# Attention, conv gate and routed attention in one kernel: P V products of both head halves as one operation in the score banks

## The chip, the cores and the metric

The kernel runs on one core of a Trainium2 chip. The metric is the device time in microseconds (us) of one execution. Three runs of the kernel before took 679.58, 679.75 and 681.16 us, so the median is 679.75.

## What is computed

Three stages follow each other, for 8 batches of 576 positions and 512 channels (cut to what matters):

```python
# 1: windowed attention, 8 heads of 64
scores = scale * q @ k.T;  mask = (rel >= 0) & (rel < 64)
attn = exp(scores - max); attn = attn / (attn.sum(-1) + 1e-9);  x = attn @ v
# 2: causal conv of 5 taps as a gate
gate = 1 / (1 + exp(-conv(x, conv_w)));  x = (gate * (x @ w_val)) @ w_out
# 3: four experts of causal attention (64 wide), the two with the largest logits kept
logits = x @ w_gate;  sel = the 2 largest of 4;  w = softmax(sel)
for e in experts:
    a = softmax(causal(scale * (x @ wq[e]) @ (x @ wk[e]).T))
    out += chosen[e] * w[e] * (a @ (x @ wv[e]) @ wo[e])
```

The kernel multiplies `w_out` into `wq`, `wk`, `wv` and `w_gate` beforehand, so stage 3 starts from the gated values.

## The kernel before

A batch is cut into five row tiles, four of 128 positions and a last one of 64. That makes forty tiles, n = 0 to 39, with j = n % 5. Each passes through the same chain of operations, which the code names by short stages:

- `qt`, `qe`: q and k are transposed on TensorE (line 669) and copied out of PSUM.
- `sp`, `mx`, `ex`, `ph`, `pl`: the scores of stage 1 (lines 728, 730), their maximum (737), the exponential (744), and probabilities as a float16 value plus a float16 remainder (`Phl`, lines 275 and 282). `PT` transposes them by DMA.
- `pv`, `xn`: the product with the values (line 794) for four heads at a time, so two halves for each tile of 128 positions and one for a last tile. `rcs` (799) and `rci` (802) make the reciprocals of the sums from column 64, and `xn` (809) multiplies by them.
- `xt`, `xT`, `xh`, `xl`: x is transposed on TensorE (829, 826) and written three ways (275, 842). GpSimd then computes the conv (861 to 872).
- `val`, `gv`, `gh`, `gl`: the product with `w_val` (890 to 892), the gate and the split. `qk` (923 to 925) and `v3` (941 to 943, 954) are the products with the folded weights, `rt` (992 to 1030) the routing.
- `s3`, `m3`, `x3`, `f3`, `ph3`, `pl3`, `P3T`: the scores of stage 3 (1073) in one or two groups, softmax, `P3hl`, DMA transpose (1118). `y` (1153) and `o` (1174, 1178 to 1180) are the two last products, `ot` and `st` the copy and the store.

Every float32 product is made of three float16 ones (high times high, high times low, low times high).

PSUM has eight banks. `sc` has two buffers of two banks for the scores of both stages, `pj` two of one bank for `val`, `qk`, `v3` and `o`, `tr` one bank for the transposes, and `o` one bank that `pv` and `y` share. A buffer is taken at an operation's first matmul and is free again when the last reader is done. For `sc` that is the `pl` or `pl3` residual on VectorE.

The order of instructions on each engine is not that of the code. A planner, the class `Plan`, runs once while the kernel is built: it holds each operation's cost, its readers and the buffers that it takes, and places operations by a due time, which is the tile's start plus the stage's entry in the table `OFF` (with `BOOST`, `EARLY` and others). What results is a fixed order on each engine, with a fixed buffer for each tile; an engine waits at an instruction whose operands are not there. `SP` issues all DMAs, loads, stores and transposes alike. At the start TensorE also gets 36 groups of filler matmuls (line 1201) while the weights load and are converted. The folded weights are scaled and split on VectorE (`sps` at 540 to 542, then the residuals `wproj<-wp,sp,wproj` at 282); `qk` of tile 0 waits for them.

Of the kernel before, what the change touches and what calls it, by code (L numbers as in the profile page):

```python
# [34 lines left out]
OFF = dict(yh=61969.4, x3=76298.1, vl=20442.0, vs=13922.2, qk=54953.8, val=50000.0, ot=20813.6, yn=88307.5, gv=18491.1,  # L35
           qt=454.3, qe=-25419.0, gl=26778.7, rt=99733.5, yl=94279.8, s3=67381.4, ex=47180.1, vh=31559.9, st=81376.7,
           xT=10029.4, dq=13818.2, xl=67807.4, am=-5435.3, ph3=58596.7, xn=-25423.0, v3h=38686.3,
           pl=23451.7, o=98000.0, ph=101124.6, pl3=67418.4, h3=52915.4, yt=64737.1, th=53943.5,
           v3l=14936.7, xt=4442.6, l3=40133.4, m3=74450.1, P3T=76142.0, sp=15925.6, ld=59750.6, pv=28118.3,
           vb=7408.6, cv=66570.7)  # L40
# [8 lines left out]
WATV = 23439.39  # L49
WATP = 61184.73  # L50
# [4 lines left out]
BOOST = {0: 49596.2, 3: 463.2, 4: -4467.5, 5: 1761.0, 7: -1392.4, 8: 4527.3}  # L55
LD0 = -175524.04
LD1 = 1628.22
ORDER = "raw0 wv0 wv3 wv2 v2 v1 v3 v0 v4 wv1 cw wo2 raw1 wo wo1 raw2 wo0 raw3 wcat raw4 wo3".split()
# [11 lines left out]
EARLY = 2.85  # L70
# [147 lines left out]
def attention_conv_moe(ctx: ExitStack, tc: tile.TileContext, q, k, v, w_val, conv_w, w_out,  # L218
# [439 lines left out]
    def attn1(n):  # L658
# [142 lines left out]
        def rci(half):  # L801
            ve.reciprocal(T_["rc", n, half], T_["rc", n, half])

        def xn(half):
            o, rc = T_["o1", n, half], T_["rc", n, half]
# [3 lines left out]
            ve.tensor_mul(dst, o[:, :, 0:64], rc[:, :, None].to_broadcast([128, 4, 64]))  # L809

        vr = [("VA", n, 0), ("VA", n, 1)] + ([("VB", n)] if j else [])
        for h in range(NB):
            op("pv", n, (("PE", (18 if j else 13) * mm(65)),), lambda h=h: pv(h), r=[("PT", n)] + vr, w=[("o1", n, h)])
            chain("xn", n, ("rc", n, h), [("DVE", lambda h=h: rcs(h)), ("DVE", lambda h=h: rci(h))], [("o1", n, h)], [])
            op("xn", n, (("DVE", dv(256)),), lambda h=h: xn(h),
               r=[("o1", n, h), ("rc", n, h, 1)] + ([("xn", n, 0)] if h else []), w=[("xn", n, h)])
# [93 lines left out]
    def proj(n):  # L910
# [73 lines left out]
        op("v3l", n, both(4, False), lg, r=[("pw", n)], w=[("w4", n, 0)])  # L984

        def rtA():
# [44 lines left out]
        op("rt", n, (("DVE", 450.0),), rtA, r=[("pw", n), ("w4", n, 0), ("scs", b, 3)], w=[("pw", n, "c"), ("w4", n, 1)])  # L1031
# [8 lines left out]
    def attn2(n):  # L1040
# [197 lines left out]
```

## Time and profile before

| what | value |
|---|---|
| median of three runs | 679.75 us |
| profiled execution, its own time | 679.55 us |
| span of its trace, first to last instruction | 677.7 us |
| PE (TensorE matmul) busy | 628.5 us, 93% |
| DVE (VectorE) busy | 557.4 us, 82% |
| ACT (ScalarE) busy | 515.6 us, 76% |
| POOL (GpSimd) busy | 483.1 us, 71% |
| DMA queue q1, share of 16 engines | 74.1% |

The ends of matmuls are modelled in the trace, so PE's busy time is an upper figure. PEld is TensorE's loading of weights, which runs beside PE. A wait is put down to the instruction that came last. Idle time of an engine that is not the bound costs nothing.

### The profile page before, as it was taken

To read this page: it belongs to the slowest core of one execution; us is meant where nothing else is said; L and a number is where in the kernel's file an instruction comes from. 1 tells how busy PE (TensorE), PEld (TensorE's weight loads), DVE (VectorE), ACT (ScalarE), POOL (GpSimd) and SP (SyncE) were. 2 spreads that over 40 slices of the span, in tenths; PEclk is the share of its full clock that TensorE was granted. 3 is DMA by queue.
4 is the path that set the end of the run, shared out by engine and by line. 5 is a ranking of instruction groups with operands and counts; after the bars stand their busy time and mean duration, and the time that the engine had idled before them with its cause. 6 is when DMAs were issued, how large, how long until landed. Compare 5 with 4: busy or idle time off the path is not lost. (4 is left out here: it accounts for less than half of the span.)

```text
span 677.7 us, 25338 instructions
## 1 busy us (share of the span) xinstructions
PE 628.5 (93%) x10225; PEld 489.9 (72%) x10237; DVE 557.4 (82%) x1695; ACT 515.6 (76%) x1340; POOL 483.1 (71%) x546
## 2 busy tenths in 40 slices
PE   8979979889999999999989999999999999999985
PEld 4436768677787778777877778777887688767753
DVE  7695697788979988998888886989789898887782
ACT  2656557877897888888797869787897888777773
POOL 4674967997596688786985879497977777973500
PEclk9989989999999999999999999999999999999998
DMA  8769952795995988967996977797686664556257
GB/s 224 188 164 194 235 114 46 163 168 107 157 223 120 173 153 139 196 129 143 162 184 142 180 134 154 156 177 150 114 172 129 96 127 111 98 114 118 43 123 145
DMA packets 306531, 99.45 MB, mean 147 GB/s; under 512 B 294362, under 2 KB 296942, under 8 KB 306414
## 3 DMA queue, kind: packets, MB, share of 16 engines
q1 hardware_dynamic: 306414, 97.84, 74.1%
q8 instruction: 80, 1.31, 0.8%
q14 instruction: 37, 0.30, 0.1%
HBM read 34.63 MB, written 9.44 MB: 65 GB/s over the span
## 5 line engine op out<-in xcount | busy, mean ns | idle before, releaser
L872 POOL TENSOR_TENSOR acc<-acc,ctmp 128x512 f32<-128x512 f32 (+1 forms) x160 | 185.9, 1162 | 6.3
L870 POOL TENSOR_TENSOR ctmp<-xT,cw 128x512 f32<-128x512 f32 (+1 forms) x160 | 151.5, 968 | 0.0
L744 ACT ACTIVATE sc<-sc,mx 128x128 f32<-128x128 f32 x288 | 99.0, 344 | 33.0 <-DVE mx L737 25.0
L890 PE MATMUL pj<-xs,wval 128*128 128x128 f16 (+1 forms) x640 | 101.1, 216 | 1.0 <-ACT k L275 1.0
L923 PE MATMUL pj<-gs,wproj 128*128 128x128 f16 (+1 forms) x640 | 101.6, 216 | 0.1
L924 PE MATMUL pj<-gs,wproj 128*128 128x128 f16 (+1 forms) x640 | 101.4, 216 | 0.0
L925 PE MATMUL pj<-gs,wproj 128*128 128x128 f16 (+1 forms) x640 | 101.4, 216 | 0.0
L891 PE MATMUL pj<-xs,wval 128*128 128x128 f16 (+1 forms) x640 | 101.0, 215 | 0.0
L892 PE MATMUL pj<-xs,wval 128*128 128x128 f16 (+1 forms) x640 | 100.9, 215 | 0.0
L1087 ACT ACTIVATE sc<-sc,mx 128x128 f32<-128x128 f32 (+3 forms) x144 | 75.9, 527 | 30.2 <-DVE mx L1082 27.3
L861 POOL TENSOR_TENSOR acc<-xT,cw 128x512 f32<-128x512 f32 (+1 forms) x31 | 31.7, 1023 | 81.9 <-issue 40.7
L282 DVE SCALAR_TENSOR_TENSOR P3hl<-sc,mx,P3hl 128x128 f16<-128x128 f32 (+3 forms) x144 | 75.8, 573 | 11.6 <-ACT P3hl L275 10.3
L275 ACT ACTIVATE P3hl<-sc,mx 128x256 f16<-128x256 f32 (+4 forms) x134 | 66.4, 564 | 8.9 <-DVE mx L1100 4.9
L1073 PE MATMUL sc<-k,q 64*128 64x128 f32 (+5 forms) x384 | 66.5, 451 | 4.9 <-DVE P3hl L282 3.5
L1082 DVE TENSOR_REDUCE mx<-sc 128x4 f32<-128x512 f32 (+3 forms) x64 | 61.5, 965 | 3.4 <-PE sc L1073 2.6
L923 PEld LDWEIGHTS <-wproj 128*128 128x128 f16 x640 | 62.1, 99 | 2.3 <-issue 0.5
L890 PEld LDWEIGHTS <-wval 128*128 128x128 f16 x640 | 61.9, 99 | 1.7 <-issue 0.9
L891 PEld LDWEIGHTS <-wval 128*128 128x128 f16 x640 | 61.9, 99 | 1.6 <-issue 1.1
L924 PEld LDWEIGHTS <-wproj 128*128 128x128 f16 x640 | 62.1, 99 | 0.5 <-issue 0.3
L925 PEld LDWEIGHTS <-wproj 128*128 128x128 f16 x640 | 62.1, 99 | 0.0
L892 PEld LDWEIGHTS <-wval 128*128 128x128 f16 x640 | 61.9, 99 | 0.0
L691 POOL TENSOR_TENSOR VA<-rv,VA 128x512 f16<-128x512 f32 (+1 forms) x40 | 45.9, 1156 | 19.5 <-ACT VA L275 11.4
(200 smaller groups left out, 1763.4 us busy)
## 6 DMA issues: line engine op xcount, KB each, us to landing
VB<-VA SPq DMA_DIRECT2D x64, 132.0 KB, 2.9
raw<-in_q SPq DMA_DIRECT2D x32, 256.0 KB, 3.9
raw<-in_k SPq DMA_DIRECT2D x32, 256.0 KB, 3.8
rv<-in_v SPq DMA_DIRECT2D x32, 256.0 KB, 3.9
out<-ot SPq DMA_DIRECT2D x32, 256.0 KB, 2.7
w<-in_moe_w_val SPq DMA_DIRECT2D x4, 512.0 KB, 5.2
w<-in_moe_w_out SPq DMA_DIRECT2D x4, 512.0 KB, 3.7
rv<-in_v SPq DMA_DIRECT2D x8, 128.0 KB, 3.5
```

Source lines behind the costliest of these rows:

```text
L282: ve.scalar_tensor_tensor(o, i, scale, hi, op0=OP.mult, op1=OP.subtract)
L744: ac.activation(ps[:, i, :], ps[:, i, :], AF.Exp, bias=t[:, hh:hh + 1])
L870: po.tensor_mul(y, x[:, :, t + i:t + i + T], W["cw"][:, :, t + i:t + i + 1].to_broadcast([128, 4, T]))
L872: po.tensor_add(acc[:, :, :T], acc[:, :, :T], y)
L890: pe.matmul(p[:, m, :T], lhsT=w0, rhs=xs[:, 0, c, :T], start=c == 0, stop=False)
L891: pe.matmul(p[:, m, :T], lhsT=w0, rhs=xs[:, 1, c, :T], start=False, stop=False)
L892: pe.matmul(p[:, m, :T], lhsT=w1, rhs=xs[:, 0, c, :T], start=False, stop=c == 3)
L923: pe.matmul(p[:, m, :T], lhsT=w0, rhs=gs[:, 0, c, :T], start=c == 0, stop=False)
L924: pe.matmul(p[:, m, :T], lhsT=w0, rhs=gs[:, 1, c, :T], start=False, stop=False)
L925: pe.matmul(p[:, m, :T], lhsT=w1, rhs=gs[:, 0, c, :T], start=False, stop=c == 3)
L1073: pe.matmul(ps[ot, c0:c0 + r.shape[-1]], lhsT=l, rhs=r, start=bk not in seen, stop=i == final[bk])
L1087: ac.activation(ps[:, x], ps[:, x], AF.Exp, bias=mx[:, x:x + 1], accum_out=mx[:, 4 + x:5 + x])
```

## The change

`pv` becomes one operation for a tile. It takes an `sc` buffer (two banks, 264 columns of one for each half) and issues the matmuls of both halves one after the other. One `rcs` and one `rci` then work on 128x8 sums, and two `xn` multiplications follow. The `o` bank is gone; its bank goes to `tr`, which now has two buffers, and `y` takes one of these. In the routing, `lg` now writes the logits already scaled, two comparisons multiply the raw ones by the same scale, and the `tensor_scalar` that scaled the maximum is gone (40 instructions). With this, most numbers of the planner's tables are new, so almost every engine's order differs.

```diff
-           P3hl=2, P3T=3, V3=7, q3=3, k3=2, ys=2, ot=1, am=2, scs=3, w4=3, sc=2, o=1, tr=1, pj=2,
+           P3hl=2, P3T=3, V3=7, q3=3, k3=2, ys=2, ot=1, am=2, scs=3, w4=3, sc=2, tr=2, pj=2,
-KIND = dict(wf=("pj", 1), kT=("kT", 1), k3=("k3", 1), qp=("tr", 2), s1p=("sc", 1), s3p=("sc", 2), o1=("o", 2), xp=("tr", 1), yp=("o", 1),
+KIND = dict(wf=("pj", 1), kT=("kT", 1), k3=("k3", 1), qp=("tr", 2), s1p=("sc", 1), s3p=("sc", 2), o1=("sc", 1), xp=("tr", 1), yp=("tr", 1),
-ORDER = "raw0 wv0 wv3 wv2 v2 v1 v3 v0 v4 wv1 cw wo2 raw1 wo wo1 raw2 wo0 raw3 wcat raw4 wo3".split()
+ORDER = "wv2 v4 wv3 raw0 v3 wv0 v1 v2 v0 wv1 cw wo2 wo raw1 raw2 wo3 wo1 wo0 raw3 wcat raw4".split()
-EARLY = 2.85
+EARLY = 3.83
...
-            o = bank(("o1", n, half), [128, 4, 66])
+            o = o1(half)
...
-        def rcs(half):
-            o = T_["o1", n, half]
-            T_["rc", n, half] = rc = pool.tile([128, 4], F32, name="rc", bufs=6)
-            ve.tensor_scalar(rc, o[:, :, 64], 1e-9 * PS, 256.0, op0=OP.add, op1=OP.mult)
+        def o1(half):
+            return T_["o1", n][:, 512 * half:512 * half + 264].rearrange("p (i d) -> p i d", d=66)
...
+        def pvs():
+            bank(("o1", n), [128, 1024])
+            for h in range(NB):
+                pv(h)
...
+        def rcs():
+            T_["rc", n] = rc = pool.tile([128, 8], F32, name="rc", bufs=4)
+            ve.tensor_scalar(rc[:, :4 * NB].rearrange("p (h i) -> p h i", h=NB)[:, :, :, None], both_halves(64, 65), 1e-9 * PS, 256.0, op0=OP.add, op1=OP.mult)
...
+        op("pv", n, (("PE", (18 if j else 13) * mm(65) * NB),), pvs, r=[("PT", n)] + vr, w=[("o1", n)])
+        chain("xn", n, ("rc", n), [("DVE", rcs), ("DVE", rci)], [("o1", n)], [])
...
-            copy(e, w4[:, 0], T_["pw", n][:, 128:132])
+            copy(e, w4[:, 0], T_["pw", n][:, 128:132], col(b, 3))
...
-            ve.tensor_tensor(r[:, :, 1], other, own, op=OP.is_equal)
-            ve.tensor_tensor(r[:, :, 0], other, own, op=OP.is_gt)
-            t = w4[:, 3]
-            ve.tensor_reduce(t[:, 0:1], w4[:, 0], axis=AX.X, op=OP.max, negate=True)
-            ve.tensor_scalar(t[:, 0:1], t[:, 0:1], col(b, 3), None, op0=OP.mult)
+            ve.scalar_tensor_tensor(r[:, :, 1], own, col(b, 3), other, op0=OP.mult, op1=OP.is_equal)
+            ve.scalar_tensor_tensor(r[:, :, 0], own, col(b, 3), other, op0=OP.mult, op1=OP.is_lt)
+            ve.tensor_reduce(w4[:, 3, 0:1], w4[:, 0], axis=AX.X, op=OP.max, negate=True)
...
-            o = bank(("yp", n), [128, 2, 128])
+            o = bank(("yp", n), [128, 4, 128])
```

Three places of the order. The first is VectorE around the `xn` of tile 18 (j = 3), before: the two halves stand five rows apart, and each has its own reciprocals.

```order
L799 TENSOR_SCALAR rc<-o 128x4
L802 RECIPROCAL rc<-rc 128x4
L809 TENSOR_TENSOR xn<-o,rc 128x4x64
L282 SCALAR_TENSOR_TENSOR P3hl<-sc,mx_6420,P3hl 128x512 x2
L907 TENSOR_TENSOR gs<-pj,gs 128x512
L799 TENSOR_SCALAR rc<-o 128x4
L282 SCALAR_TENSOR_TENSOR Phl<-sc,Phl 128x512
L802 RECIPROCAL rc<-rc 128x4
L809 TENSOR_TENSOR xn<-o,rc 128x4x64
```

The same tile in the changed kernel reads from an `sc` buffer:

```order
L809 TENSOR_SCALAR rc<-sc 128x8
L277 COPY kT<-tr 128x4x64
L812 RECIPROCAL rc<-rc 128x8
L907 SCALAR_TENSOR_TENSOR pj<-acc,pj 128x512
L818 TENSOR_TENSOR xn<-sc,rc 128x4x64
L282 SCALAR_TENSOR_TENSOR P3hl<-sc,mx_6375,P3hl 128x512 x2
L818 TENSOR_TENSOR xn<-sc,rc 128x4x64
```

One chain of reciprocals serves both halves, and four other VectorE instructions stand between its first step and its last.

The second place is TensorE just before the first `qk` (tile 0). Before, the second half of tile 3's `pv` stands directly ahead of it:

```order
L794 MATMUL o<-VB,PT 64x65
L794 LDWEIGHTS PT
L794 MATMUL o<-VA_105,PT 64x65
L923 LDWEIGHTS wproj
L923 MATMUL pj<-gs,wproj 128x128
```

In the changed kernel the `pv` of tile 5 and transposes for tiles 8 and 9 stand there:

```order
L797 MATMUL sc<-VA_103,PT 128x65
L669 MATMUL tr<-ident,raw 128x128 x4
L669 MATMUL tr<-ident,raw 128x64 x4
L932 LDWEIGHTS wproj
L932 MATMUL pj<-gs,wproj 128x128
```

Ahead of the first `qk` TensorE now has two more `val`, two more `xt`, one more `sp`, five more `qt` and three more halves of `pv`; the filler groups and the weight products ahead of it are the same in number.

The third place is VectorE where the scale of the folded weights is made (540 to 542, `sps`). Before, it follows the `xn` of tile 2's first half:

```order
L593 TENSOR_REDUCE am<-rv 64x1
L809 TENSOR_TENSOR xn<-o,rc 128x4x64
L540 TENSOR_REDUCE cm<-sc 128x2
L541 TENSOR_REDUCE cm<-sc 128x1
L542 TENSOR_REDUCE cm<-sc 128x1
```

In the changed kernel it follows tile 3's two `xn` and the `Phl` residual of tile 5:

```order
L812 RECIPROCAL rc<-rc 128x8
L818 TENSOR_TENSOR xn<-sc,rc 128x4x64 x2
L282 SCALAR_TENSOR_TENSOR Phl<-sc,Phl 128x1024
L540 TENSOR_REDUCE cm<-sc 128x2
L541 TENSOR_REDUCE cm<-sc 128x1
L542 TENSOR_REDUCE cm<-sc 128x1
```

So more of the attention's VectorE work stands ahead of the scale than before.

## Rows read from the trace of the kernel before

**Rows 1.** Busy time by stage: us, busy (x count) by engine, clock, DMA, GB/s.

```profile
0.00:99.85 99.85, 85.36 (x734) 54.05 (x742) 74.00 (x148) 55.34 (x112) 63.73 (x73) 0.97 0.81 190
99.85:160.00 60.15, 53.13 (x885) 45.63 (x880) 47.90 (x153) 44.59 (x122) 51.84 (x56) 0.93 0.58 110
160.00:640.00 480.00, 462.91 (x8207) 373.64 (x8212) 412.47 (x1322) 394.27 (x1053) 367.03 (x414) 1.00 0.77 144
640.00:677.70 37.70, 27.08 (x413) 16.60 (x409) 23.02 (x75) 21.41 (x54) 0.47 (x4) 0.91 0.60 123
```

**Rows 2.** Waits of PE: who waited <- for whom: us, times, longest.

```profile
PE o L794 <- DVE xn L809: 4.5, 3, 4.0
PE sc L1073 <- DVE P3hl L282: 3.5, 5, 1.2
...
PE tr L471 <- DVE kT L277: 3.0, 1, 3.0
PE sc L728 <- DVE P3hl L282: 2.2, 3, 0.9
PE o L794 <- DVE ys L282: 2.0, 2, 1.5
...
PE tr L669 <- DVE cw L422: 1.6, 1, 1.6
...
PE tr L669 <- DVE xs L842: 1.4, 2, 0.9
PE sc L1073 <- DVE Phl L282: 1.1, 2, 0.6
```

**Rows 3.** VectorE by line and shape: out<-in, count | busy us, mean ns | idle before.

```profile
L802 DVE RECIPROCAL rc<-rc 128x4 f32<-128x4 f32 x72 | 12.3, 171 | 0.6
L799 DVE TENSOR_SCALAR rc<-o 128x4 f32<-128x4 f32 x72 | 11.0, 153 | 9.4 <-PE o L794 9.3
...
L996 DVE TENSOR_SCALAR w<-w,sc_d 128x1 f32<-128x1 f32 x40 | 8.6, 214 | 1.4
```

**Rows 4.** PE in order of time around one half of `pv`: start, us, instruction.

```profile
71.15 0.22 PE L891 MATMUL pj<-xs,wval 128*128 128x128 f16 x1
71.20 0.22 PE L892 MATMUL pj<-xs,wval 128*128 128x128 f16 x1
71.35 0.22 PE L794 MATMUL o<-VB,PT 128*64 128x65 f16 x1
...
71.73 0.20 PE L794 MATMUL o<-VA,PT 128*64 128x65 f16 x1
71.85 0.46 PE L669 MATMUL tr<-ident,raw 64*128 64x64 f32 x4
```

**Rows 5.** PE and DVE in order of time: three score buffers, taken and left.

```profile
192.15 0.41 PE L728 MATMUL sc<-band_middle,twice 64*64 64x512 bf16 x4
200.80 1.22 DVE L282 SCALAR_TENSOR_TENSOR Phl<-sc,Phl 128x1024 f16<-128x1024 f32 x1
309.36 1.13 PE L1073 MATMUL sc<-k,q 64*128 64x512 f32 x4
317.77 1.41 DVE L282 SCALAR_TENSOR_TENSOR P3hl<-sc,mx,P3hl 128x512 f16<-128x512 f32 x2 [0.27 <-ACT P3hl L275]
319.69 0.15 DVE L799 TENSOR_SCALAR rc<-o 128x4 f32<-128x4 f32 x1
320.56 0.42 DVE L809 TENSOR_TENSOR xn<-o,rc 128x256 f32<-128x256 f32 x1
```

**Rows 6.** DVE and PE in order of time around the first `qk`.

```profile
92.86 3.93 DVE L282 SCALAR_TENSOR_TENSOR wproj<-wp,sp,wproj 128x1024 f16<-128x1024 f32 x3
99.15 1.25 DVE L282 SCALAR_TENSOR_TENSOR wproj<-wp,sp,wproj 128x16 f16<-128x16 f32 x1
99.28 0.26 PE L794 MATMUL o<-VB,PT 128*64 128x65 f16 x1 [3.97 <-DVE xn L809]
100.09 0.29 PE L923 MATMUL pj<-gs,wproj 128*128 128x128 f16 x1
```

More of the change, by code (lines that the diff above doesn't have):

```diff
@@ L34 @@
 STRETCH = 1.5
[L35 to L40, printed above, removed]
+OFF = dict(yh=95028.9, x3=58485.9, vl=27701.0, vs=15833.9, qk=54891.8, val=50000.0, ot=17870.6, yn=68299.7, gv=39579.3,
+           qt=7471.7, qe=-30431.1, gl=-10171.5, rt=126820.9, yl=96093.9, s3=65757.9, ex=50963.8, vh=25037.0, st=58132.7,
+           xT=5135.7, dq=-26951.7, xl=78861.1, am=20771.4, ph3=54843.6, xn=-72068.1, v3h=28271.5,
+           pl=4407.2, o=98000.0, ph=110490.4, pl3=19948.2, h3=62034.2, yt=91047.1, th=36540.8,
+           v3l=-2146.2, xt=-32396.0, l3=31033.0, m3=68081.1, P3T=110794.1, sp=16066.3, ld=-2495.8, pv=28118.3,
+           vb=6688.8, cv=65589.8)
 SMALL = 70.0
@@ L48 @@
 C3Q = ("SP",)
-WATV = 23439.39
-WATP = 61184.73
+WATV = 56082.99
+WATP = 81622.45
 DMA_A = 650.0
@@ L794, in pv, with both_halves, rci @@
                         pe.matmul(o[qs, i, 0:65], lhsT=pt[:, a, hh, qs], rhs=vt[:, c, h, 0:65], start=a + c == 0, stop=a == 1)
[L796 to L802 removed]
+        def pvs():
+            bank(("o1", n), [128, 1024])
+            for h in range(NB):
+                pv(h)
+        def both_halves(d0, d1):
+            return T_["o1", n].rearrange("p (h x) -> p h x", h=2)[:, :NB, :264].rearrange("p h (i d) -> p h i d", d=66)[:, :, :, d0:d1]
+        def rcs():
+            T_["rc", n] = rc = pool.tile([128, 8], F32, name="rc", bufs=4)
+            ve.tensor_scalar(rc[:, :4 * NB].rearrange("p (h i) -> p h i", h=NB)[:, :, :, None], both_halves(64, 65), 1e-9 * PS, 256.0, op0=OP.add, op1=OP.mult)
+        def rci():
+            ve.reciprocal(T_["rc", n][:, :4 * NB], T_["rc", n][:, :4 * NB])
         def xn(half):
[L805 removed]
             if ("xn", n) not in T_:
@@ L808, in xn @@
             dst = T_["xn", n][:, 0:4] if last else T_["xn", n][:, half::2]
-            ve.tensor_mul(dst, o[:, :, 0:64], rc[:, :, None].to_broadcast([128, 4, 64]))
+            ve.tensor_mul(dst, o1(half)[:, :, 0:64], T_["rc", n][:, 4 * half:4 * half + 4, None].to_broadcast([128, 4, 64]))
         vr = [("VA", n, 0), ("VA", n, 1)] + ([("VB", n)] if j else [])
+        op("pv", n, (("PE", (18 if j else 13) * mm(65) * NB),), pvs, r=[("PT", n)] + vr, w=[("o1", n)])
+        chain("xn", n, ("rc", n), [("DVE", rcs), ("DVE", rci)], [("o1", n)], [])
         for h in range(NB):
-            op("pv", n, (("PE", (18 if j else 13) * mm(65)),), lambda h=h: pv(h), r=[("PT", n)] + vr, w=[("o1", n, h)])
-            chain("xn", n, ("rc", n, h), [("DVE", lambda h=h: rcs(h)), ("DVE", lambda h=h: rci(h))], [("o1", n, h)], [])
             op("xn", n, (("DVE", dv(256)),), lambda h=h: xn(h),
-               r=[("o1", n, h), ("rc", n, h, 1)] + ([("xn", n, 0)] if h else []), w=[("xn", n, h)])
+               r=[("o1", n), ("rc", n, 1)] + ([("xn", n, 0)] if h else []), w=[("xn", n, h)])
         def xt():
@@ L983, in proj @@
         op("v3l", n, (("DVE", dv(256)),), v3l, r=[("pw", n), ("V3", n, 0)], w=[("V3", n, 1)])
-        op("v3l", n, both(4, False), lg, r=[("pw", n)], w=[("w4", n, 0)])
+        op("v3l", n, both(4, False), lg, r=[("pw", n), ("scs", b, 3)], w=[("w4", n, 0)])
         def rtA():
@@ L1007, in rtC @@
             w4 = T_["w4", n]
-            ac.activation(w4[:, 1], w4[:, 0], AF.Exp, bias=w4[:, 3, 0:1], scale=col(b, 3))
+            ac.activation(w4[:, 1], w4[:, 0], AF.Exp, bias=w4[:, 3, 0:1])
         def rtF():
@@ L1030, in rtI @@
             ve.tensor_scalar(w4[:, 4], T_["pw", n][:, 264:268], w4[:, 3, 2:3], None, op0=OP.mult)
-        op("rt", n, (("DVE", 450.0),), rtA, r=[("pw", n), ("w4", n, 0), ("scs", b, 3)], w=[("pw", n, "c"), ("w4", n, 1)])
+        op("rt", n, (("DVE", 400.0),), rtA, r=[("pw", n), ("w4", n, 0), ("scs", b, 3)], w=[("pw", n, "c"), ("w4", n, 1)])
         op("rt", n, (("ACT", 190.0),), rtC, r=[("w4", n, 1)], w=[("w4", n, 2)])
@@ L1158, in yh @@
         def yh(e):
-            copy(e, new(("ys", n), [128, 2, 2, 128], F16, late())[:, 0, :, :T], T_["yp", n][:, :, :T], 1.0 / PS)
+            copy(e, new(("ys", n), [128, 2, 2, 128], F16, late())[:, 0, :, :T], T_["yp", n][:, 0:2, :T], 1.0 / PS)
         op("yh", n, both(2 * T, False), yh, r=[("yp", n)], w=[("ys", n, 0)])
@@ L1163, in yl @@
             ys = T_["ys", n]
-            residual(ys[:, 1, :, :T], T_["yp", n][:, :, :T], ys[:, 0, :, :T], 1.0 / PS)
+            residual(ys[:, 1, :, :T], T_["yp", n][:, 0:2, :T], ys[:, 0, :, :T], 1.0 / PS)
         op("yl", n, (("DVE", dv(2 * T)),), yl, r=[("yp", n), ("ys", n, 0)], w=[("ys", n, 1)])
```

6 lines of the change are left out of this document (3 added, 3 removed).

## Prediction

> **What bounds the kernel now.** I read the busy time of the engines by stage first, then the list of waits, then single stretches in order of time. The stages [rows 1] show where TensorE is the bound and where it is not. From 160 to 640 us PE is busy 462.91 of 480.00 us: 17.1 us idle, 3.6%, so no change there can win more than that without making PE's own work shorter. In the first 99.85 us it is busy 85.36 us, but part of this is filler, so the real work waits for weights and for the first tiles. VectorE is the next engine (412.47 of 480.00, 86%), ScalarE follows (82%). Making either faster moves the end only as far as a wait of PE ends earlier.
>
> The list of PE's waits [rows 2] then says what PE waits for. Three kinds matter here. Waits for the single buffers of `o` and `tr`, which the change does away with: 4.5 us for an `xn` that still reads `o` (one of them 4.0), 2.0 for a `ys` residual on `o`, 3.0 for a copy by VectorE out of `tr`, 1.6 for another, 1.4 for an `xs` residual on `tr`; 12.5 us in all. Waits for the score buffers: 3.5 + 2.2 + 1.1 = 6.8 us. The rest are data, and the change leaves them in place.
>
> **The sum.** It is made against the profiled execution, 679.55 us, which is 1.85 us above its span and 0.2 us under the median of 679.75; a difference of that size is not spoken of below.
>
> VectorE's instructions. One chain of reciprocals for a tile of 128 positions takes away 32 of 72 `rcs` and 32 of 72 `rci`: 32 x (0.153 + 0.171) = 10.4 us [rows 3]. The 40 scalings of the routing's maximum go as well: 40 x 0.214 = 8.6 us [rows 3]. The remaining chains are 8 columns wide and not 4, and two comparisons take a scale; of these forms there is no row, and I bound them by 0 and by the 0.04 us that lie between the 153 and the 214 ns of the small instructions shown, for 112 instructions at most 5 us. So VectorE has 14 to 19 us less of 557. I cost that at 0 on the end, since PE's work covers it; it is used below as slack in the handing over of buffers. If PE were not the cover, the cost of a queue on VectorE would show there.
>
> The Trainium skill (Perfetto Trace Analysis, Optimizing Scalar/DVE Operations) puts the overhead of a VectorE instruction at about 60 ns from SBUF and 125 ns from PSUM. By it the 32 + 32 + 40 instructions are worth 32 x 0.125 + 72 x 0.060 = 8.3 us of engine time, an estimate, where the rows give 19.0; by either the end does not move.
>
> Joining the halves. At one half of `pv` the step into it is 71.35 - 71.20 = 0.15 us where the matmuls before it follow at 0.05, and the step out of it 71.85 - 71.73 = 0.12 where its own follow at about 0.03 [rows 4]: 0.10 + 0.09 us of change-over. In 31 of 32 tiles other work stood between the halves. A join removes both steps but leaves one between the neighbours. I take 0.10 each, 31 x 0.10 = 3 us won; ends: 0, and 31 x 0.19 = 6.
>
> Buffers of `tr` and `y`, past the first 100 us. Of the 12.5 us, 4.5 - 4.0 = 0.5, 2.0 and 1.4 lie there: 3.9 us [rows 2]. What comes late next is mostly the same consumer's other operand, so I take 3 us won; ends 0 and 3.9.
>
> The start. The other 8.6 us (4.0 + 3.0 + 1.6) lie before the first `qk` [rows 2]. The 4.0 us end at 99.28, and the folded weights' last residual runs from 99.15 to 100.40, beside a `qk` that starts at 100.09 [rows 6]. So the wait for `o` goes, but the weights are late next: freeing that buffer alone wins nothing. What wins is the new order. Ahead of the first `qk` stand two more `val`, 2 x 48 x 0.055 = 5.3 us [rows 4], and five `qt`, two `xt`, three halves of `pv` at about 0.5 each (0.46 and 0.50 in [rows 4]), and an `sp` taken as two of these: 6 us. That is 11 us of work done while the weights are made. Against it the scale stands behind the residual of tile 5 on VectorE, and the loads of raw q and k come behind three other transfers, so the first `qk` will not start at 100 us again. If it starts at 111, nothing is won; if at 100, 11. VectorE is idle for 99.85 - 74.00 = 25.9 us of this stretch [rows 1], enough to take about 11 us more, but much of that idleness is chains, so I take the middle: `qk` at 105, 6 us won; ends 0 and 11.
>
> The clock. In 99.85 to 160 the granted clock averages 0.93 [rows 1], a stretch that follows a wait of 3.97 us [rows 6]: at that average 0.07 x 60.15 = 4.2 us are lost against full speed. With that wait filled half may come back: 2 us won, ends 0 and 4.
>
> The score buffers. This is the price. A buffer with stage-1 scores is held from 192.15 to 202.02, 9.9 us, one with stage-3 scores from 309.36 to 319.18, 9.8 us [rows 5]. A tile has one of the first and on average 64/40 = 1.6 of the second, so each of the two buffers is held (9.9 + 1.6 x 9.8)/2 = 12.8 us for each tile, of a pace of (677.70 - 99.85)/40 = 14.4 us [rows 1]: 89%. A joined `pv` holds one for 1.0 us of matmuls and 1.3 to 1.9 of chain (0.15 + 0.17 + 2 x 0.42 = 1.2 at best; a single half took 319.69 to 320.98, 1.3 [rows 5]), say 2.9. That adds 1.45: 14.25 of 14.4, 99%. In the trace 104 takings cost 6.8 us of PE, 0.065 each. With 144 at the same rate the waits grow by 2.6 us, at twice the rate by 12. I take 6 us lost: the `pl` and `pl3` chains will come round sooner with 19 us less on VectorE. Ends 0, and 20 by the first rival.
>
> Together: - 3 - 3 - 6 - 2 + 6 = - 8, so 671.6, as predicted time 672 us. The likeliest case itself, with one term or another off, spans 666 to 677.
>
> **Rivals.** First, the score buffers set the pace: slower. Mechanism: a tile's `pv` stands in the two buffers between the scores of two stages, and the last reader of each is one VectorE instruction in a fixed queue. For it speaks the 99% above, and that PE's waits for `sc` are already 6.8 us at 89%. Against it, holds are partly queueing and shorten when VectorE has less. Point from which it decides: a hold longer by 0.5 us, about one `xn` of 0.42 [rows 5] more between a maximum and its residual. Then a tile needs (10.4 + 1.6 x 10.3)/2 + 1.45 = 14.9, 0.5 more than the pace, 40 x 0.5 = 20 us, less the 8 of joining, buffers and part of the start: 679.6 + 20 - 8 = about 691 us. The Trainium skill (Perfetto Trace Analysis, Matmuls) says that independent groups of matmuls should rotate through different PSUM banks, so that emptying one overlaps the next group; by it the transposes gain and the scores lose, and which wins is what this trace leaves open.
>
> Second, the waits change their names: no difference. The 12.5 us were waits that hid others, chiefly the weights and the transposed probabilities. For it speaks the residual that ends just as `qk` starts [rows 6]. Then the start wins 0 to 2, the joining 3, and the score buffers take 3: 678 to 680 us.
>
> Third, the start goes all the way: `qk` at 100 us, no loss at the score buffers: 679.6 - 3 - 3 - 11 - 4 + 2 = about 661 us.
>
> **Chances.** The forecast 0.44, the score buffers 0.25, the waits renamed 0.18, the start in full 0.13. A difference under 0.3%, 2 us, cannot be told from none. The forecast and the third rival are faster, 0.57; of the second about three quarters lie within 2 us, 0.13, and the rest is split. Of the rival on the other side some lies close to the line. So faster 0.59, same 0.13, slower 0.28. The range leaves out the far half of the third case and the far third of the first rival: 662 to 689.
>
> **What would show it.** In the profile after: no PE wait for an `xn` or a `ys` residual on `o`, and those for `tr` near 1 us; if they stay, the second buffer did nothing. The first `qk` between 100 and 111 us. PE's waits on `sc` between 7 and 19 us, 13 in the forecast; above 25 the first rival holds. PE's idle time from 160 to 640, 17.1 us before, between 15 and 22. VectorE's busy time 538 to 543 us. The granted clock after the first `qk` at 0.96 or more. The prediction is wrong in its mechanism if the time falls with the start no earlier, or rises with the waits on `sc` no longer.

## The result, and the profile after

After takes 688.50 us (median of 4 runs, 686.99 to 690.20) against 679.66 us (4 runs, 676.27 to 681.16) of before on the same chip: ratio 1.0144, 95% interval 1.0105 to 1.0183. It is slower by about 9 us; 672 was forecast, and 688.5 lies at the upper end of the range. The profiled execution took 690.2 us with a span of 688.4, 10.7 us more than the span of before.

Where the 10.7 us are, by stages of after, in the columns of [rows 1]:

```profile
0.00:99.85 99.85, 88.62 (x810) 56.92 (x812) 69.79 (x135) 57.65 (x123) 68.65 (x81) 1.00 0.81 193
99.85:160.00 60.15, 51.31 (x845) 42.58 (x845) 53.76 (x161) 46.93 (x127) 50.61 (x53) 0.94 0.58 122
160.00:640.00 480.00, 447.58 (x8007) 361.26 (x8001) 403.22 (x1214) 373.34 (x984) 357.95 (x404) 1.00 0.72 141
```

Up to 160 us PE is busy for 88.62 + 51.31 = 139.9 us, against 138.5 of [rows 1]: 1.4 us less waiting at the start. The granted clock counts as well. It averages 1.00 and 0.94 in the two stages, against 0.97 and 0.93 before, so by these means about 3 us less of PE's busy time was lost at the lower of its two levels (1.2 and not 2.4 GHz), an estimate. From 160 to 640 PE is idle for 32.4 us, against 17.1: the loss, 15.3 us, lies in the steady stretch. Over the whole span PE's busy time is 625.2 us, against 628.5, 3.3 us less. Not all of this is the joining: before, 15.1 us of PE's busy time ran at the lower level, in after 10.0, which explains up to half the difference, 2.5 us. The spans thus differ by - 1.4 (idle to 160) + 15.3 (idle from 160 to 640) + 0.1 (idle behind) - 3.3 (busy) = + 10.7 us.

What PE waits for in after, as in [rows 2]:

```profile
PE tr L1161 <- DMA P3T<-P3hl: 5.8, 5, 2.2
PE sc L1081 <- DVE P3hl L282: 5.5, 10, 1.1
PE tr L669 <- ACT qT L275: 5.3, 2, 5.2
PE sc L797 <- DMA PT<-Phl: 3.9, 3, 1.8
...
PE sc L728 <- DVE P3hl L282: 3.3, 3, 1.6
PE pj L932 <- DVE gs L916: 3.2, 4, 1.5
...
PE sc L797 <- DVE Phl L282: 1.7, 2, 1.2
...
PE sc L1081 <- DVE rc L809: 1.6, 1, 1.6
...
PE sc L797 <- DVE P3hl L282: 1.3, 4, 0.6
PE sc L1081 <- DVE Phl L282: 1.1, 1, 1.1
```

The waits for an `xn` or a `ys` on `o` [rows 2] are gone. In their place stand waits for a score buffer that a VectorE instruction still reads. Summed over the whole list, PE's waits on `sc` that VectorE ends grew from 7.0 to 16.7 us (2.2 us for the operand `kT`, L730, are not in the 16.7), those on `o` and `tr` together fell from 26.2 to 18.8, and all of PE's waits grew from 43.2 to 57.7. That is 14.5 more, less the 3.3 of busy time: 11.2, the difference of the spans to half a microsecond. Below, "waits on `sc`" or on `tr` are such sums of all rows with that output, whatever ended them; by that count after has 26.1 on `sc` and 18.8 on `tr`, before 7.7 on `sc`.

Where the 15.3 us were lost, the same list for 160 to 640 us alone tells best. The first rows of the `sc`, `o` and `tr` buffers, before and then after:

```profile
PE o L794 <- DMA PT<-Phl: 2.9, 4, 1.1
...
PE sc L728 <- DVE P3hl L282: 1.3, 2, 0.7
PE sc L1073 <- DVE Phl L282: 1.1, 2, 0.6
```

```profile
PE sc L797 <- DMA PT<-Phl: 3.9, 3, 1.8
PE tr L1161 <- DMA P3T<-P3hl: 3.5, 4, 1.1
PE sc L728 <- DVE P3hl L282: 3.3, 3, 1.6
PE sc L1081 <- DVE P3hl L282: 3.0, 6, 1.1
PE sc L797 <- issue: 1.7, 1, 1.7
...
PE sc L1081 <- DVE rc L809: 1.6, 1, 1.6
```

By buffer, the waits on `sc` grew from 4.1 to 19.2 us in this stretch, those on `o` and `tr` went from 8.6 to 7.8, those on `pj` from 3.0 to 4.6. By operation, since `pv` moved from `o` to `sc`: the scores waited 10.2 us, against 4.1, `pv` (L794, now L797) 9.0, against 4.0, and all that goes into `tr` 7.8, against 4.6. Of the 19.2 on `sc`, 12.2 were ended by VectorE (3.6 before) and 3.9 by the transposed probabilities, an operand of `pv`, for which it waited 2.9 before, on `o`. So nearly the whole loss stands at the score buffers.

VectorE has 556.9 us of work, against 557.4, where 538 to 543 were forecast. By line:

```profile
L279 DVE TENSOR_SCALAR Phl<-sc 128x1024 f16<-128x1024 f32 (+1 forms) x9 | 10.4, 1159 | 2.5 <-ACT w L1016 1.3 <-ACT sc L744 1.2
...
L1003 DVE SCALAR_TENSOR_TENSOR pj<-pj,sc_d,w 128x16 f32<-128x16 f32 x40 | 9.7, 243 | 1.4
L1002 DVE SCALAR_TENSOR_TENSOR pj<-pj,sc_d,w 128x16 f32<-128x16 f32 x40 | 9.5, 236 | 7.1 <-ACT V L275 6.6
...
L812 DVE RECIPROCAL rc<-rc 128x8 f32<-128x8 f32 (+1 forms) x40 | 7.6, 191 | 0.4
...
L809 DVE TENSOR_SCALAR rc<-sc 128x8 f32<-128x8 f32 (+1 forms) x40 | 6.4, 159 | 10.3 <-PE sc L797 10.1
```

The chains went from 23.3 us [rows 3] to 14.0 and the 40 scalings of 8.6 are gone; but the two comparisons with a scale take 236 and 243 ns, 5 us more in all than the comparisons of before (174 and 179 ns), and the new order put more copies on VectorE: nine of the stage-1 probabilities, 10.4 us, against four of 4.4. ScalarE has 508.3 us, against 515.6.

The start, in order of time (start, us, engine, instruction, wait):

```profile
98.46 1.22 DVE L282 SCALAR_TENSOR_TENSOR Phl<-sc,Phl 128x1024 f16<-128x1024 f32 x1 [3.95 <-ACT Phl L275]
99.60 0.68 DVE L540 TENSOR_REDUCE cm<-sc 128x2 f32<-128x512 f32 x1
...
103.80 8.28 DVE L282 SCALAR_TENSOR_TENSOR wproj<-wp,sp,wproj 128x1024 f16<-128x1024 f32 x5
112.01 0.68 DVE L907 SCALAR_TENSOR_TENSOR pj<-acc,pj 128x512 f32<-128x512 f32 x1
...
113.86 0.69 PE L669 MATMUL tr<-ident,raw 64*128 64x64 f32 x4 [5.19 <-ACT qT L275]
114.61 0.27 PE L932 MATMUL pj<-gs,wproj 128*128 128x128 f16 x1
```

The reduction `cm` at L540 begins the scale of the folded weights. Before, the same instruction stands here:

```profile
88.07 0.67 DVE L540 TENSOR_REDUCE cm<-sc 128x2 f32<-128x512 f32 x1
```

The first `qk` starts at 114.6 us, not at 105 (before: 100.1, [rows 6]). Of these 14.5 us 11.5 are there already at the scale: it stands behind the residual of tile 5, and for that VectorE's queue waited 3.95 us, until ScalarE had made its copy. The weights' five residuals take until 112, much as long as before (92.86 to 100.40). The rest comes behind them: a gating product that waits there holds up ScalarE, and ScalarE the copy that frees PE's `tr` buffer.

### The profile page after: what moved, and what is told of

Same layout as the page of the kernel before. It is cut to its first block, busy times and chain, and to the rows that moved or that the text cites. A ratio compares the mean times of both kernels' runs of the same rounds, so it can differ in the third digit from the quotient of the medians.

```text
span 688.4 us, 25226 instructions
## 1 busy us (share of the span) xinstructions
PE 625.2 (91%) x10237; PEld 486.4 (71%) x10237; DVE 556.9 (81%) x1607; ACT 508.3 (74%) x1312; POOL 483.4 (70%) x549
## 5 line engine op out<-in xcount | busy, mean ns | idle before, releaser
L899 PE MATMUL pj<-xs,wval 128*128 128x128 f16 (+1 forms) x640 | 99.7, 214 | 1.7 <-ACT k L275 1.1
L901 PE MATMUL pj<-xs,wval 128*128 128x128 f16 (+1 forms) x640 | 99.4, 214 | 0.0
L900 PE MATMUL pj<-xs,wval 128*128 128x128 f16 (+1 forms) x640 | 99.4, 214 | 0.0
L1095 ACT ACTIVATE sc<-sc,mx 128x128 f32<-128x128 f32 (+3 forms) x144 | 76.0, 527 | 26.1 <-DVE mx L1090 23.3
L282 DVE SCALAR_TENSOR_TENSOR P3hl<-sc,mx,P3hl 128x128 f16<-128x128 f32 (+3 forms) x144 | 75.8, 573 | 11.6 <-ACT P3hl L275 10.6
L275 ACT ACTIVATE P3hl<-sc,mx 128x384 f16<-128x384 f32 (+4 forms) x131 | 66.3, 572 | 18.1 <-DVE mx L1108 5.4
L870 POOL TENSOR_TENSOR acc<-xT,cw 128x512 f32<-128x512 f32 (+1 forms) x34 | 33.5, 985 | 50.9 <-issue 26.2
```

The source lines that it names most:

```text
L275: ac.activation(o, i, AF.Copy, scale=scale)
L282: ve.scalar_tensor_tensor(o, i, scale, hi, op0=OP.mult, op1=OP.subtract)
L899: pe.matmul(p[:, m, :T], lhsT=w0, rhs=xs[:, 0, c, :T], start=c == 0, stop=False)
L900: pe.matmul(p[:, m, :T], lhsT=w0, rhs=xs[:, 1, c, :T], start=False, stop=False)
L901: pe.matmul(p[:, m, :T], lhsT=w1, rhs=xs[:, 0, c, :T], start=False, stop=c == 3)
L1095: ac.activation(ps[:, x], ps[:, x], AF.Exp, bias=mx[:, x:x + 1], accum_out=mx[:, 4 + x:5 + x])
```

## The experiments

The theory at first (T): each taking of a score buffer by a joined `pv` costs waits, some 10 us in all. Rivals: the new tables of numbers give a worse order (A); VectorE, with dearer comparisons and more copies, is the limit (B); and, after the first four runs, (C): each order fits its own buffers, and wherever the product stands in it something waits. From e5 on, and in e1, the order of operations stands in the kernel as a list, taken from before or after, in place of the planner. Ratios are to before, run on the same chip; after is 1.0144. A difference to after is the difference of the two ratios times 680 us. An operation whose buffer is not free at its place in the list comes later. So some orders are kept nearly and not wholly: 16 operations of PE came late in e5, 19 in e6 (and 40 of VectorE), 9 in e11, 5 in e13, 16 in e17 and 5 in e18; in e1, e7 to e10, e12 and e14 to e16 the order is kept.

**e1: the pool of two alone**, in the order of before.

```diff
-sc=2, o=1, tr=1      o1=("o", 2)   yp=("o", 1)
+sc=2, tr=2           o1=("tr", 2)  yp=("tr", 1)
```

> The kernel before, instruction for instruction in its own order; only the buffers differ: o and tr are one pool of two, and each half of a P V product takes one of them, so does y. Theory (the joined P V in the score banks costs about 10 us): the tr and o waits past the start go (3.9 us), score waits stay near 7 us, so 676 us (674 to 680). Rival A (the new tables of numbers cost it: a later start, a later y): also about 676, since the order is before's. Rival B (VectorE is loaded no less and its comparisons cost more): nothing of it is here, so 676 to 680 as well. Above 682 all three are wrong on the buffers.

680.63 us, ratio 1.0012 (0.9979 to 1.0045). Nothing won: PE's waits on `o` and `tr`, 26.2 us before, are 24.7 us on `tr` now. The 3 us that the forecast took for these buffers are not there. Of its 12.5 us of named waits 8.4 still stand, now on `tr` (`xn` 2.8, `ys` 2.3, `kT` 3.3), and the wait for `P3T` grew from 1.9 to 4.2 us. But in e1 the halves of `pv` stand in the pool too, which they don't in after; a pool of two without them, in before's order, was not run.

**e2 to e4: tables and code crossed**, the planner making the order anew. e2 is after with each half in a `tr` buffer and a chain of its own:

```diff
-o1=("sc", 1)
+o1=("tr", 2)
```

e3 is before with after's tables (`OFF`, `WATV`, `WATP`, `BOOST`, `LD0`, `LD1`, `ORDER`, `EARLY`), e4 after with before's.

> The kernel after with one thing undone: each half of a P V product is an operation of its own again, with its own chain of reciprocals, in one of the two tr buffers; the score buffers hold scores alone. The tables of numbers, the routing's comparisons and the pool of two stay as after. Theory: 688.5 - 10 (score waits back from about 17 to about 7 us) + 3 (the joining undone) = 681 us (678 to 684). Rival A (tables): the late start and the late y stay, so 688 to 692. Rival B (VectorE): 72 chains again, 10 us more of VectorE, so 689 to 694.

> The kernel before with the tables of numbers of after (due times, order of the loads) and nothing else; the planner makes a new order. Theory: the score waits stay near 7 us, but y comes late as after (+4) and the start is no earlier: 680 to 686 us. Rival A (tables): it is these that cost the 9 us, so 688 to 692. Rival B (VectorE's comparisons): 680.

> The kernel after with the tables of numbers of before; joined P V in the score banks, pool of two and comparisons stay. Theory: the score waits are there under any tables, 15 to 25 us: 687 to 696 us. Rival A (tables): back to before or better, 674 to 682 us. Rival B: as after, 686 to 690.

e2: 700.37 us, 1.0292 (1.0242 to 1.0342). e3: 720.18, 1.0582 (1.0523 to 1.0640). e4: 713.17, 1.0485 (1.0423 to 1.0546). All three are slower than either kernel, and than any case that was expected. Waits on `sc` are 9.2 and 7.3 us where the banks hold scores alone (e2, e3) and 31.1 in e4, as T would have it; but e2, which undoes just that, is 10 us slower than after, with 36.3 us on `tr`. Tables and code belong together, and taking one back cannot price the other. Hence the runs with the order kept.

**e5, e13: the product out of the score banks, in after's order.** In e5 two halves in `tr`, without the second half's sums; in e13 (without the first half's sums and values) both halves written over each other into one `tr` buffer.

```diff
 e5:  -bank(("o1", n), [128, 1024])      +bank(("o1", n, half), [128, 512])   # tr
 e13: -bank(("o1", n), [128, 1024])      +bank(("o1", n), [128, 512])         # tr
      -T_["o1", n][:, 512 * half:...]    +T_["o1", n][:, :264]
```

> The order of after kept (an operation stands later only where its buffer is not free), its tables, comparisons and pool of two; undone is the use of the score banks alone: the halves of P V stand one behind the other on TensorE and each takes a tr buffer. One chain of reciprocals for the first half's sums serves both halves, so VectorE's instructions stay as many (the second half's sums are left out). Theory (score banks cost about 10 us): score waits fall from about 17 to about 7 us and the time to 676 - 682 us. Rival A (the order of after: start, y): 686 to 691 us, what leaves the score waits comes back elsewhere. Rival C (nothing single: each order fits its own buffers, as the two kernels with crossed tables suggest): 690 to 705 us, with waits for tr.

> After in its own order (one or two operations stand later), all instructions as after, but the joined P V does not go into a score buffer: both halves are written over each other into one tr buffer and both xn read it (the first half's sums and values are left out). Theory S (it is the taking of score buffers that costs): score waits of 24 us fall to 12 or less and tr waits grow less than that: 677 to 683 us. Theory C (the product has to stand somewhere, and wherever it stands in this order something waits): 688 to 700 us, tr waits up by 10 us or more.

e5: 715.87 us, 1.0522 (1.0456 to 1.0589). e13: 697.22, 1.0238 (1.0209 to 1.0266). The waits on `sc` fall from 26.1 to 12.9 and 11.4 us, as T says, and those on `tr` rise from 18.8 to 41.5 and 30.3; `pj` takes its share too. C holds: of the three places tried in this order the score banks come out best, though they cost; e5, above even what C expected, and e13 have some operations late as well. The first rows of e13's list of waits:

```profile
PE pj L992 <- DVE gs L976: 8.3, 5, 2.9
PE tr L1221 <- DMA P3T<-P3hl: 5.8, 5, 2.2
PE sc L1141 <- DVE P3hl L342: 5.0, 8, 1.1
PE tr L898 <- DVE xn L878: 4.3, 5, 1.5
```

**e6, e14: joining in before's order.** e6 has the whole code of after, score banks included; e14 joins too, but into the one `o` buffer, with the halves over each other, so that the first half's values are left out. In outline:

```diff
 e6:  SEQ = order of before, the joined pv at the place of the first half
 e14: the same, and   -sc=2, tr=2   +sc=2, o=1, tr=1   o1=("o", 1), yp=("o", 1)
```

> The reverse: all of the change but its tables, in the order of before (the joined P V at the place of the first half; an operation stands later only where its buffer is not free). Theory: +10 us of score waits, -3 of joining: 685 to 692 us. Rival A (the tables' order is what costs): 674 to 680 us. Rival C: 695 to 715 us, waits for score buffers of 25 us and more.

> Joining by itself in the order of before: one operation and one chain in each tile, into the single o buffer of before with the halves written over each other (the first half's values are left out), and the comparisons of after; score buffers, tr and tables as before. The forecast's term: 3 us won, 677 us (674 to 680). If the place of an operation in a fitted order matters more than its length: 684 us or more.

e6: 735.96 us, 1.0830 (1.0785 to 1.0876). e14: 678.33, 0.9952 (0.9925 to 0.9979). The two differ in where the product and `y` are written, in the halves that lie over each other in e14, and in the operations that came late in e6, nine of its `pv` among them, by two to four places; in time by some 60 us. e6 is above every case that was expected. e14 is the one kernel faster than before whose interval excludes none, by 3.3 us, near the 3 forecast; but its VectorE has 551.1 us of work, 6.3 less than before, and so more than the joining differs. PE's busy time is 625.7 us, 2.8 less than before, of which the clock explains some 1.1. In e6 PE waits on `sc` for 63.3 us; the first rows of its list:

```profile
PE sc L1140 <- DVE xn L877: 18.2, 17, 2.3
PE sc L856 <- DVE P3hl L341: 13.2, 9, 2.6
PE sc L856 <- DVE Phl L341: 7.8, 6, 2.8
PE sc L787 <- DVE xn L877: 4.8, 4, 1.8
```

So joining pays a little at most, and its place takes it back. After's order was fitted to that place: there the loss against before is some 9 us, not the 56 of e6.

What a join is worth on PE can be read from the matmuls themselves, where neither a wait nor the lower clock disturbs them: from the start of the last matmul ahead of `pv` to the start of the first one behind, a half of 24 matmuls takes 0.65 us (median, before) and a joined `pv` of 48 takes 1.04 (after). That is 0.26 less than two halves, less the one step of some 0.1 that the neighbours of the half keep.

**e7, e8: a longer hold, and the same work without it**, in after's order.

```diff
             ve.tensor_mul(dst, o1(half)[:, :, 0:64], rc...)
+            if half == NB - 1: ve.tensor_mul(spare, o1(half)[:, :, 0:64], rc...)   # e8: spare, dst
```

> After in its own order, with one more VectorE instruction in each tile that reads the second half of P V out of the score buffer into a spare tile, so that the buffer is held 0.42 us longer and VectorE has 40 x 0.42 = 17 us more. Theory: the handing over of score buffers is what TensorE waits for, so of 17 us about half or more comes through against the next kernel: 5 to 12 us above it. Rival B (VectorE is the limit): the same time as the next kernel within 2 us, both 8 us or more above after.

> The same instruction at the same place, but reading the tile that the one before it wrote, not the score buffer, so the buffer is let go as in after. Theory: VectorE's 17 us more cost 0 to 5 us over 688.5. Rival B: 8 to 17 us over.

e7: 695.63 us, 1.0228 (1.0182 to 1.0274). e8: 700.67, 1.0308 (1.0257 to 1.0358). The rows of the added instruction, e7 and then e8:

```profile
L881 DVE TENSOR_TENSOR spare<-sc,rc 128x256 f32<-128x256 f32 x40 | 16.5, 414 | 0.0
```

```profile
L881 DVE TENSOR_TENSOR spare<-xn,rc 128x256 f32<-128x256 f32 x40 | 25.4, 635 | 1.4
```

The control was not equal: from SBUF the instruction takes 635 ns, not 414. Nor is that SBUF alone: in the ten instances of e8 beside which GpSimd was idle for four fifths of the time or more it took 424 to 426 ns, and among the others up to 1462; in e7 all 40 took 407 to 418. Per microsecond of VectorE both cost much the same, 5.7 of 16.5 (0.35) and 11.2 of 25.4 (0.44), each cost uncertain by some 4 us. So with this control the longer hold shows no price of its own, against T, though a small one would not be seen; added VectorE work does, but not in full, against B.

**e9, e10: less VectorE work**, in after's and in before's order.

```diff
-ve.tensor_reduce(am, T_["rv", n][:T].rearrange("p h d -> p (h d)"), ...)
+ve.tensor_reduce(am, T_["rv", n][:T].rearrange("p h d -> p (h d)")[:, :128], ...)
```

> After in its own order; the absolute maximum of v reads a quarter of its columns, so that VectorE has about 40 x 0.5 = 20 us less (three quarters of v are left out of the maximum). Theory V (each us of VectorE moves the end by about 0.4 us, as the two kernels with a spare instruction had it: 16.5 us for 6, 25.4 us for 11): 678 to 683 us. Theory H (the handing over of score buffers is a matter of the order on TensorE, VectorE's slack does not help): 686 to 689 us.

> The same quarter in the kernel before, in its own order. If VectorE's load is paid in both kernels alike: 671 to 675 us. If only the shared score buffers made it be paid, as theory H with VectorE as the releaser would have it: 677 to 680 us, no difference.

e9: 687.02 us, 1.0112 (1.0038 to 1.0185). e10: 679.14, 0.9973 (0.9936 to 1.0010). VectorE's work is 540.7 us in e9 (after: 556.9) and 542.6 in e10 (before: 557.4). The stretch from 160 to 640 us, in the columns of [rows 1], in e9 and then in e10:

```profile
160.00:640.00 480.00, 450.23 (x8095) 364.73 (x8095) 398.91 (x1224) 376.64 (x995) 362.12 (x410) 1.00 0.73 142
```

```profile
160.00:640.00 480.00, 460.04 (x8132) 370.97 (x8136) 400.99 (x1305) 390.40 (x1043) 363.97 (x411) 0.99 0.76 142
```

So 15 to 16 us less VectorE work are worth some 2 us in either kernel, and the intervals hold none as well; e9's reaches to a gain of 7. PE's idle time in this stretch is 29.8 us in e9, against 32.4. So B, and with it the missing relief on VectorE, doesn't explain the loss: here work added to a fitted order cost, and work taken away gave little.

**e11, e12: after's order mended by hand.** In e11 19 operations of PE are to go ahead of one that waited, such as `v3` 8 before `pv` 11. In e12 the nine copies of probabilities go back to ScalarE. In outline:

```diff
 e11: -pv 11, v3 8   +v3 8, pv 11      (19 such places)
 e12: -ph on DVE     +ph on ACT        (9 tiles)
```

> After with 19 operations on TensorE moved up by one to three places, each ahead of one that waited 0.46 to 1.8 us (pv 8, pv 11, s3 4, sp 19 and so on; together 19 us of waits), all else in the same order. Theory H (a wait in the queue while other work stood ready): 678 to 684 us. Theory V (TensorE waits for VectorE's stream, so what is moved up only lets the wait turn up later): 686 to 692 us.

> After in its own order, but the nine conversions of probabilities (128 x 1024) that the new order had put on VectorE run on ScalarE, at the same places: VectorE 10.4 us less, ScalarE 9.2 us more. Theory V: 683 to 686 us. Theory H: 687 to 691 us. If ScalarE is as tight as VectorE: above 691.

e11: 709.29 us, 1.0420 (1.0358 to 1.0481). e12: 695.78, 1.0249 (1.0164 to 1.0333). e11 is above both its cases. Only 15 of the 19 moves came about, some by fewer places: `val` 6, `o` 4, `v3` 15 and `xt` 31 fell back, since their buffers were not free, so it was not shown that ready work stood behind the waits. It cost 19 us more than after. PE's waits on `pj` rose from 12.8 to 22.7 us, and part of the loss is the clock: its mean is 0.975, against 0.990, and PE's busy time 632.8 us, against 625.2. The likeliest reason for the rest, not tested: what was moved up came before its own data, or took a buffer that the next one needed. In e12 VectorE has 11.6 us less (545.3), ScalarE 7.1 more (515.4), and the time is 7 us longer: the third case, above 691, which was put down to ScalarE being as tight as VectorE.

**e15, e16: shorter chains behind the scores**, in after's and in before's order.

```diff
-ve.tensor_reduce(mx[:, :NX], view(g), op=OP.max, negate=True)
+ve.tensor_reduce(spare[:, :NX], W["p"][:, 0, :NX, :wd], op=OP.max, negate=True)
-ac.activation(..., AF.Exp, bias=mx[:, x:x + 1], ...)
+ac.activation(..., AF.Exp, bias=zero[:, 0:1], ...)
```

> After in its own order; the maximum of the stage-3 scores no longer stands between TensorE and the exponential: VectorE runs a reduction of the same size over weights, the exponential takes a zero bias (the subtraction of the maximum is left out). 64 holds of a score buffer become shorter by about 1 us each, with VectorE's work the same. Theory S: shorter holds pay in after, 676 to 682 us. Theory C: 686 to 690.

> The same in the kernel before. Theory S: its score buffers are not the limit, so it wins at most a third of what after wins: 677 to 680 us. Theory C: 677 to 681, as much or little as after.

e15: 700.59 us, 1.0293 (1.0262 to 1.0324). e16: 681.87, 1.0003 (0.9984 to 1.0022). The maximum of the scores is left out of both. Neither gains, e15 lies above all its cases, and the reason is worth more than the times: the holds did not shorten. Over the tiles 8 to 34 a stage-3 buffer is held for 8.85 us in after and 8.86 in e15, 9.90 and 9.85 in before and e16. One of them, PE's taking and VectorE's last reading, in after:

```profile
431.55 1.13 PE L1081 MATMUL sc<-k,q 64*128 64x256 f32 x8 [0.23 <-DVE P3hl L282]
...
433.14 1.21 DVE L1090 TENSOR_REDUCE mx<-sc 128x4 f32<-128x1024 f32 x1
...
440.67 1.21 DVE L737 TENSOR_REDUCE mx<-sc 128x8 f32<-128x1024 f32 x1
441.80 1.65 DVE L282 SCALAR_TENSOR_TENSOR P3hl<-sc,mx,P3hl 128x256 f16<-128x256 f32 x4
```

and the same in e15, where the exponential no longer waits for the reduction:

```profile
444.36 1.21 DVE L1153 TENSOR_REDUCE spare<-wproj 128x4 f32<-128x1024 f16 x1
...
452.02 1.22 DVE L800 TENSOR_REDUCE mx<-sc 128x8 f32<-128x1024 f32 x1
453.15 1.65 DVE L342 SCALAR_TENSOR_TENSOR P3hl<-sc,mx,P3hl 128x256 f16<-128x256 f32 x4
```

From the reduction's start to the end of the residual it is 10.3 us in after and 10.4 in e15. Between them VectorE works off other tiles' instructions almost without a gap, and the residual comes when the queue reaches it. The chain itself was hardly shorter: over these tiles the exponential began 2.66 us after the first matmul of its scores, against 3.09 in after, and the 0.43 us are found again as a longer wait between its end and the residual (3.67 us, against 3.24). Why e15 lost 10 us where e16 lost none isn't settled. Half of it is PE's busy time, 630.0 us against 625.2, at a mean clock of 0.978 against 0.990; its waits grew as well, from 57.7 to 64.1 us.

**e17, e18: joining with the whole computation and no score banks**: before's order, both halves one behind the other, in a pool of two `tr` buffers, at the place of the first or of the second half. In outline:

```diff
-pv(n, 0) ... xn(n, 0) ... pv(n, 1) ... xn(n, 1)
+pv(n, 0) pv(n, 1) ... xn(n, 0) xn(n, 1)
```

> The kernel before in its own order with both halves of P V one behind the other at the place of the first, each with its own chain, in a pool of two tr buffers that o, tr and y share; the whole computation, no score bank. Theory (joining is worth 3 us by its change-overs, the score banks and the new order lose it): 676 to 680 us, the first kernel faster than before with the whole computation. If two buffers for transposes, halves and y are too few, as in the two kernels that took the halves out of the score banks: 683 us or more, tr waits above 30 us.

> The same at the place of the second half: xn comes later, so the transposes of x stand closer behind it. Theory: 677 to 682 us; an xt that waits for xn would cost up to 32 x 0.4 = 13 us more.

e17: 704.85 us, 1.0350 (1.0322 to 1.0378). e18: 696.75, 1.0228 (1.0191 to 1.0266). Waits on `tr` are 32.6 and 30.2 us, and the rival of e17's expectation holds: two buffers are too few. Next to e14 the whole product needs two buffers at a time, and these two have none to spare. No kernel with the whole computation beat before.

## Why the prediction was wrong, by its own steps

*Joining, - 3.* The price holds: 0.26 us less for a joined product than for two halves, less the 0.1 kept, is 0.10 each or somewhat more. The sums agree with it but don't prove it: the clock may explain 2.5 of the 3.3 us less busy time, and e14's 3.3 us come with less VectorE work.

*The score buffers, + 6.* This step failed, and counted by buffer it is the largest error. The place was right and the direction too, the price was not. From 160 to 640 us the waits on `sc` grew by 15.1 us, 8.6 of them ended by VectorE's readers; with `pv` counted by operation, 6.1 for the scores and 5.0 for `pv`. Over the whole trace the waits that VectorE ends are 16.7 us, inside the 7 to 19 named but above the 13 of the forecast; all waits on `sc` are 26.1, above the 25 at which the first rival was to hold (20.0 without the 6.1 us of waits for the operands `PT` and `kT`).

The price came from the 99% of fullness, and that did not come about. Counted from the first product to the last reader, the two buffers were held for about 86% of the stretch before and 88% in after. A joined `pv` held one for 3.2 us, near the 2.9 of the forecast, but a stage-3 hold fell from 9.90 to 8.85 us and a stage-1 hold from about 9.4 to 9.1. So the holds shortened, as the forecast said against its rival, though VectorE got none of the relief that was to do it. And yet the waits grew, from 0.07 us for each of 104 takings to 0.12 for each of 144, where the forecast took the old 0.065 or up to twice as much. Fullness was thus no measure of the waits. A hold was taken as a chain, to be cut by shorter chains; e15 and e16 show that it lasts until VectorE's queue reaches the residual. Why the waits grew in buffers hardly fuller than before stays open: the product in the score banks and the order that goes with it were not separated, since e5, e13 and e6 also have operations late.

The first rival, at 691, had the time nearly right by luck: its mechanism, holds longer by 0.5 us, isn't there. What e7 added to `pv`'s hold, about 0.4 us, showed no price beside the work.

*Buffers of `tr` and `y`, - 3.* This step failed too. The named waits went in after but for 1.6 us for a copy out of `tr`, and other waits took their place, the second rival's case. From 160 to 640 us the waits on `o` and `tr` fell by 0.8 us in all, and without `pv` they grew by 3.2. `y` waited 3.5 us there for `P3T`; over the whole span the wait for `P3T` grew from 1.9 to 5.8 us, since `y` stands closer behind its scores in the new order: it starts 7.1 us after their last residual, against 11.3 before (tiles 8 to 34). e1, with `pv` in the same pool, does not price this term.

*The start, - 6, and the clock, - 2.* PE waited 1.4 us less by 160 us, and the clock gave back about 3, so some 4 to 5 us came of the 8. The clock's part came from the wrong stage: 1.00 after 0.97 in the first 99.85 us, and only 0.94 after 0.93 behind, where the 2 us were forecast. The forecast itself said that nothing is won with the first `qk` at 111; it came at 114.6, because the scale came 11.5 us later, behind the residual of tile 5. That was the risk it had named, and it took the middle between 100 and 111 all the same, for which no row spoke: VectorE's 25.9 idle microseconds were a sum, and one wait of 3.95 us in its queue counted. A reading was wrong besides: the residual that "ends just as `qk` starts" ends at 100.40 us, after the start of `qk` at 100.09 [rows 6], so `qk` did not wait for it.

*VectorE's relief, 0 on the end.* The price agrees with the runs (some 2 us for 15 to 16, none within the intervals of e9 and e10), the amount was wrong: 0.5 us and not 14 to 19. Instruction times from rows overlap in the queue, so their sum is not engine time: in the hold shown for after, a reduction ends at 440.67 + 1.21 = 441.88 us and the residual behind it starts at 441.80. And e14, with the joining's instructions and before's choice of engines, has 6.3 us less. The two comparisons were bounded by 40 ns more each; they took some 60. The order put five more copies of probabilities on VectorE, 6.0 us, which gave back the rest; they stood in the order's rows and were not counted.

Of the signs that the forecast named, two came: no waits for `xn` or `ys` on `o` (and 1.6 us of those named on `tr`, where near 1 was forecast), and 16.7 within 7 to 19. The others did not: `qk` at 114.6 (100 to 111), 32.4 us idle (15 to 22), VectorE at 556.9 (538 to 543), the clock at 0.94 (0.96).

The Trainium skill (Perfetto Trace Analysis, Matmuls) has independent groups of matmuls rotate through different PSUM banks, so that emptying one overlaps the next group. No run here shows a gain from it: a second `tr` buffer gave 1.0012 (e1), and the joined product in the score banks cost some 60 us between e14 and e6, where operations came late as well. The Trainium skill (Perfetto Trace Analysis, Optimization Strategy) says that consistent bubbles, the same gap repeating, can mean that SBUF or PSUM has no room for the next tile. Here no single gap repeats, the largest row being 3.9 of 31.6 us from 160 to 640, but 19.2 of these us stand at the two score buffers, against 4.1 of 15.7 before, and the buffers were held for 88% of the time.

What stays open: whether an order fitted longer would bring after below before, and whether the waits come from sharing the banks or from the order. e11 and e12 show that simple mending doesn't help, and e2 to e4 that tables fitted to other code can cost 20 to 40 us. The 9 us are thus those of two fitted orders; of the buffers' part, only the direction, the place and the waits are shown.

## What to carry to other kernels

Before joining two operations, ask where the larger result stands. PE gains the change-over, but with all banks of PSUM taken each place tried here for the whole product cost more than that, and a buffer was held until the queue of its last reader reached it: a shorter chain in front of the reader did not shorten the hold (e15, e16). How full the buffers are did not tell how long PE would wait for them.

In a kernel whose order is fitted to its buffers, a wait removed is no gain until a run with the order kept shows it. In this one case the forecast's gains from waits came to little and its loss to more than twice the term. Judge a part of such a change with the order written out, and count which operations came late all the same; with the order made anew, the crossed parts ran 3 to 6% slower than before. And read a start by the queue that holds its last operand, in order of time, not by the idle time of an engine.

## Not expected of the hardware

- A VectorE product of 128x256 f32 with a broadcast factor took 407 to 418 ns with its source in PSUM (e7). With its source in SBUF it took 424 to 426 ns where GpSimd was idle beside it for four fifths of the time or more, and among the other 30 instances up to 1462 (e8).
- A reduction of 128x1024 takes the same 1.21 us from f32 in PSUM and from f16 in SBUF (1.218 and 1.210 us, after and e15).
